# First four heads of a fused attention and MLP-Mixer kernel: loaded and scored in two pairs

## The chip, the cores and the metric

The kernel runs on one core of one Trainium2 chip. The metric is the device time in microseconds of one execution, the median of several runs; lower is better. The engines are TensorE (PE, with its weight loads as PEld), VectorE (DVE), ScalarE (ACT), GpSimd (POOL) and SyncE (SP), each with an instruction queue of its own.

## The reference

Eight batches of eight heads, 576 rows, 64 columns a head. Attention is causal by blocks of 64; its output, heads side by side (512 columns), goes through a token MLP with residual and then a channel MLP with residual. All inputs and the output are float32.

```python
scores = scale * np.matmul(q, k.transpose(0, 1, 3, 2))       # (8, 8, 576, 576)
scores = np.where(block_i >= block_j, scores, -1e9)          # blocks of 64
attn = np.exp(scores - scores.max(-1, keepdims=True))
attn = attn / (attn.sum(-1, keepdims=True) + 1e-09)
x = np.matmul(attn, v)            # then heads side by side: (8, 576, 512)
h = np.maximum(x.transpose(0, 2, 1) @ w_tok1, 0.0) @ w_tok2  # 576 -> 256 -> 576
u = x + h.transpose(0, 2, 1)
out = u + np.maximum(u @ w_ch1, 0.0) @ w_ch2                 # 512 -> 1536 -> 512
```

## The kernel before

The program is a list of steps, each made by `P.add` with an engine, a cost, the steps that it depends on and the PSUM banks that it takes and gives back. The order in which they stand on the engines was planned beforehand and is written out in a long string, `ORDER`: each word is a step's number, a letter for its engine (T for PE, A for ACT, D for DVE, P for POOL, S for SP) and letters for its banks. Nothing is reordered on the chip: each engine takes its steps in this order and waits for what a step needs.

For a batch and a group of four heads (`hg` 0 or 1), `load_qk` brings keys and queries into `qk_sb` as bfloat16, one head in 32 partitions (each partition holds 18 rows of the head). GpSimd's DMAs convert from float32 on the way. A transpose on DVE (32 by 32 blocks) then gives `kT` and `qT`. `score_set` forms one of three sets of score columns for several heads; each head works in its own 32 rows of TensorE. ACT takes the exponential of a set into `e_sb`. `tail` copies and clears the columns beyond the diagonal. `head_out` and `ends_out` multiply by the values, whose last column of ones gives the sums; DVE divides. Then come `token_up`, `first_uT` or `token_mix`, `channel_up` (or forms of it with seven products in place of eight) and the down projections, `first_down` for batch 0.

Batch 0 opens the program. Here is what stands at its start:

- `raise_clock` has PE multiply zeros, eleven times 512 columns (`WARM`), and then, where the plan has PE wait, 256 columns at a time (`KEEP`; 32 of them are in the order).
- The keys of the first four heads are loaded by SP as float32 in two pieces of nine blocks into a staging area in `gT` and cast by ACT (L395); their queries are loaded by GpSimd in three pieces (L431). Five transposes (L436) follow.
- `first_attention` scores the four heads of the first set at once; later sets are scored for two heads. The exponentials of two heads are one instruction on 1024 columns (L578), except two single ones (L728).
- GpSimd's queue issues, in order: the second group's queries and keys (L431), the next batch's (L413), values (L462), the token weights (L473), the identity matrix (`masks.py`), the channel weights `wc1_sb` (L496), and later `wc2_sb` (L505) among the loads of later batches. Memsets of the values' pad columns are on DVE.
- `channel_up` of batch 0 is one step of four matmuls for each of twelve tiles.

Of the kernel before, what the change touches and what calls it, by code (L numbers as in the profile page):

```python
# [27 lines left out]
class Plan:  # L28


    TURN = {
# [22 lines left out]
    def add(  # L54
# [4 lines left out]
        o = Op()  # L59
# [3 lines left out]
        o.mode, o.at, o.urgent, o.until, o.quick, o.stick = mode, at, urgent, until, quick, stick  # L63
        o.deps = list({id(d): d for d in deps if d is not None}.values())
# [33 lines left out]
    13S 9D 5D 16S 1D 43Ta 21P 2D 7D 11D 19P 10D 4D 3D 23P 31P 29P 14A 25P 15D 17A 33P 22D 18D 27P 20D 44Tb 249P 45Tb  # L98
    46Tb 47Td 24D 48Ta 49Ta 37P 50Ta 173Tsbc 36P 179Tt 174A 51Ta 52Ta 35P 53Ta 54Ta 55Ta 56Ta 57Ta 180A 34P 175D
    177Ts 26D 58Ta 59Ta 30D 176P 60Ta 178A 198Tt 252P 32D 61Ta 62Ta 40P 63Ta 199A 64Ta 28D 196Ts 42P 65Ta 66Ta 67Ta  # L100
    197A 230Tt 251D 258P 68Ta 69Ta 250D 70Ta 192A 39P 71Ta 211Ts 231A 189Td 38P 185Ta 186T 190D 181Tb 191D 182T 193A
    41P 232D 215Tt 212A 194D 154P 195D 72Tc 183D 73Tc 184D 200Td 74Tc 216A 75Tc 157P 213D 217Ts 8D 233D 254D 155P
    201T 218A 234Tt 187D 188D 12P 204Tb 214D 253D 205T 235A 255P 236Ts 206D 207D 156P 202D 227Ta 237A 203D 208Tb
    160P 223Tc 228D 224T 229D 219Td 159P 220T 225D 278Taefg 226D 161P 209D 210D 246Tc 221D 158P 222D 238Tb 281A 239T
    247D 162P 248D 242Td 279A 243T 240D 336Tc 163P 241D 282A 244D 334Ta 245D 280A 165P 260D 338Tb 335D 273Tdhfg 256D
    339A 342Ta 276A 340Tb 164P 277A 348Te 343T 341D 275A 337D 349T 399P 257D 351Tb 352T 350A 259D 263P 345Tc 344A
    346T 353D 274A 266Tfghe 262P 347D 267A 298Tabdc 261P 268A 356Tf 302A 265P 301A 360Tc 300A 357D 269A 358Td 361A
    354Tb 299A 270A 310Tcagf 355D 362Th 313A 271D 303D 272P 304D 312A 330D 264P 364Tb 363A 314A 396P 376Ta 311A 166P
    331D 370Te 359A 402P 365A 167P 305Tcdgh 371A 377D 366Tb 405P 309A 6D 168P 400D 308A 368Ta 401D 307A 306A 292Tf
    321Td 369A 293D 289Te 294D 286Tc 367A 322D 324Th 323D 374Tf 290D 291D 287D 288D 315Td 375A 325D 372Te 326D 398D  # L110
    283Tc 397D 373A 327Th 295Ta 316D 317D 570P 425Tbgfe 296D 328D 409P 329D 318Td 284D 427A 285D 387Th 319D 583P
    426A 320D 297D 428A 332D 420Tcdbg 410P 429A 388T 424A 412P 423A 479Ta 333D 408P 422A 421A 411P 477Tb 404D
    413Tdcfe 585P 478D 391Tg 414A 403D 415A 407D 573P 392T 417A 406D 480A 169D 586P 393T 416A 576P 485Tb 572D
    457Tdcae 486D 378Tf 458A 170D 461A 389T 459A 171D 460A 379T 172D 390A 445Tbdca 418D 394D 487Te 446A 419D 481Th
    448A 488D 380T 449A 482D 447A 430Tb 571D 452Tcage 431D 442Td 432D 734P 456A 450D 436Th 381D 579P 455A 433Tb
    495Te 454A 483Tf 434D 435D 491Tg 453A 443D 382Ta 444D 437D 492A 451D 575D 439Tb 484D 471Td 497Tg 496D 493Tc 440D
    468Tf 498A 441D 383T 472D 574D 494D 384T 438D 469D 470D 587Tbceg 577D 385A 489Th 501D 590A 578D 474Tf 589A 465Ta
    473D 591A 740P 462Te 475D 476D 505Tcd 588A 466D 737P 463D 467D 506Tf 490A 582P 592D 520Tbg 464D 508A 502D 521Ta
    584P 507A 511T 523A 522D 499Te 509Th 512A 500D 526T 580D 510A 599Teacf 503D 527A 513T 593D 504D 603A 515T 581D
    602A 524Tb 514D 601A 651Tf 516D 600A 525A 517D 594Tcahe 652D 528T 596A 739D 530T 595A 738D 518T 598A 653Ta 529D  # L120
    904P 597A 519D 535Tcb 531D 654A 619Tdfeh 735D 538A 533T 623A 736D 539Ta 622A 534D 536Th 901P 621A 541T 540D 743P
    620A 613Te 537D 659Tg 542A 624P 545T 614D 532A 615D 750P 626Tdcfh 660D 604Te 749P 546D 629A 661Tg 605D 628A 543T
    606D 630A 548T 662D 655Te 627A 544D 664S 631Tcfhg 549A 625D 547D 657Td 656D 632A 607Ta 633A 610Tb 658D 554Tce
    635A 608D 611D 663S 634A 612D 609D 616Tb 550D 555A 648Ta 763Tdfgh 551D 386S 556T 766A 395S 552D 765A 764A 560T
    553D 767A 557D 758Tdgfh 649D 650D 642Tc 759A 558Ta 643D 760A 741D 761A 644D 617D 645Td 762A 618D 669Tgc 665D
    646D 639Tb 647D 672A 684Tfh 640D 670Td 641D 559D 675T 671A 636Tb 745D 562T 676A 917P 744D 687A 666D 916P 561D
    690T 673Td 563D 747P 691A 564T 637D 674A 638D 568S 913P 667D 742D 751Tbagf 746P 565D 677T 914P 752A 679T 753A
    678D 566T 915P 754A 680D 755A 748P 795Tbadg 567D 756P 815Tf 907P 799A 668D 905D 798A 910P 688Te 902D 797A 685Td
    903D 796A 817Ta 689A 816D 686D 692T 818A 694T 693D 681A 783Tbdgf 695D 821Ta 785A 757D 819Te 822D 786A 682T 787A
    825Td 820D 699Tag 683A 826D 829S 823Tf 784A 777Tc 702A 824D 774Td 788P 697T 789P 778D 705T 779D 698A 775D 771Tb  # L130
# [1435 lines left out]
```

## Time and profile before

| | us |
|---|---|
| Median of three runs | 284.93 (284.62 to 286.27) |
| Profiled execution, its own time | 285.06 |
| Its span in the profile | 283.0 |
| PE busy | 275.3 |
| DVE busy | 245.1 |
| ACT busy | 172.3 |
| POOL busy | 69.3 |

The span is the time from the first to the last instruction; some 2 us lie around it. Times in the views are microseconds from the start of the span. In the chain of waits a row is start, length and what ran. In the timeline a row is start, length, engine, line, operation, output and input tile, shapes and count, and in brackets how long the engine was idle before it and what ended that. Rows of groups give, after the bar, the busy time and the mean of one in nanoseconds, then the idle time before them. Rows of DMA issues end with the us from issue to landing.

### The profile page before, as it was taken

How to read it: one execution, taken by the hardware profiler on the slowest of the kernel's cores; microseconds unless marked ns; L12 is line 12 of the kernel's file. 1: busy time of each engine (PE TensorE's matmuls, PEld its weight loads, DVE VectorE, ACT ScalarE, POOL GpSimd, SP SyncE). 2: the span in 40 equal slices, each digit the busy share in tenths (PEclk: the TensorE clock that was granted, in tenths of full speed). 3: DMA queues.
4: the chain of work that ended last, by engine and by line, in shares of the span. 5: the costliest groups of instructions: out<-in, count | busy, mean ns of one | idle time of the engine just before them, and what ended most of it. 6: DMA issues, size and time to landing. Idle time of an engine off the chain costs nothing.

```text
span 283.0 us, 9371 instructions
## 1 busy us (share of the span) xinstructions
PE 275.3 (97%) x4004; PEld 196.2 (69%) x4027; DVE 245.1 (87%) x533; ACT 172.3 (61%) x312; POOL 69.3 (24%) x115
## 2 busy tenths in 40 slices
PE   7899999999999999999999999999999999999995
PEld 3567565567776877887877767744488985468884
DVE  4678479799999988999999988899699898899975
ACT  3786887575998659787879687164514245734000
POOL 6895555511241090040535110000000000000000
PEclk9999999999999999999999999999999999999999
DMA  7999999994959599668599494030115603000436
GB/s 160 155 157 195 192 164 209 170 126 77 122 80 157 155 137 155 152 104 105 81 121 102 60 193 92 2 148 0 21 37 142 120 2 121 29 2 0 151 76 220
DMA packets 64776, 31.79 MB, mean 112 GB/s; under 512 B 53088, under 2 KB 55904, under 8 KB 64736
## 3 DMA queue, kind: packets, MB, share of 16 engines
q0 software_dynamic: 45040, 17.64, 54.0%
q1 hardware_dynamic: 19120, 12.78, 18.1%
q10 hardware_dynamic: 576, 0.79, 0.8%
q8 instruction: 31, 0.51, 0.7%
q14 instruction: 9, 0.07, 0.1%
HBM read 35.85 MB, written 9.44 MB: 160 GB/s over the span
## 4 chain that ended last, share of the span: by engine, by line
PE 85%; DMA 7%; POOL 3%; DVE 2%; issue 1%; ACT 0%; SPq 0%; DVEq 0%; POOLq 0%
PE late L1348 16%; PE mm L1348 10%; PE mm L1090 7%; PE late L1214 7%; PE late L1090 7%; PE mm L1214 6%; PE mm L560 6%; PE mm L608 4%; DMA wc_sb<-in_moe_w_ch_dram 4%; PE mm L802 3%; PE late L1443 2%; POOL vals L462 2%; PE mm L897 2%; PE late L608 2%; DMA vals<-in_v_dram 2%; PE mm L661 2%
## 5 line engine op out<-in xcount | busy, mean ns | idle before, releaser
L767 ACT ACTIVATE e_sb<-late 128x512 bf16<-128x512 f32 x85 | 48.4, 605 | 10.7 <-PE late L560 9.4
L767 ACT ACTIVATE e_sb<-mm 128x512 bf16<-128x512 f32 x83 | 47.1, 606 | 9.5 <-PE late L560 8.3
L436 DVE STREAM_TRANSPOSE qk_sb<-qk_sb 128x288 int32<-128x288 int32 (+1 forms) x65 | 41.3, 692 | 3.6 <-ACT qk_sb L395 1.9
L462 POOL DMA_DIRECT2D vals<-in_v_dram x45 | 36.8, 831 | 21.0 <-PE mm L661 8.8
L1348 PEld LDWEIGHTS <-gT 128*128 128x128 bf16 x288 | 27.7, 98 | 5.3 <-issue 0.9
L1348 PEld LDWEIGHTS <-sums 128*128 128x128 bf16 x288 | 27.7, 98 | 3.9 <-issue 0.7
L560 PEld LDWEIGHTS <-qk_sb 32*64 32x64 bf16 x1280 | 19.5, 104 | 13.7 <-issue 9.9
L560 PE MATMUL mm<-qk_sb 32*64 32x64 bf16 (+7 forms) x584 | 27.8, 287 | 0.3
L608 PEld LDWEIGHTS <-e_sb 128*128 128x128 bf16 x640 | 23.7, 97 | 5.1 <-issue 1.1
L560 PE MATMUL late<-qk_sb 32*64 32x512 bf16 (+7 forms) x556 | 26.4, 295 | 0.0
L1090 PEld LDWEIGHTS <-ws_sb 128*128 128x128 bf16 x192 | 18.2, 98 | 3.6 <-issue 0.9
L608 PE MATMUL mm<-vals,e_sb 128*128 128x65 bf16 x450 | 20.1, 193 | 0.1
L634 DVE TENSOR_TENSOR x_sb<-mm,rinv 128x256 bf16<-128x256 f32 x45 | 18.8, 422 | 1.3
L395 ACT COPY mm<-late 128x512 f32<-128x512 f32 (+1 forms) x15 | 8.7, 577 | 16.4 <-PE late L1348 8.0
L1348 PE MATMUL late<-wd_sb,gT 128*128 128x256 bf16 x144 | 17.7, 273 | 0.0
L1214 PEld LDWEIGHTS <-ws_sb 128*128 128x128 bf16 x96 | 9.3, 98 | 10.1 <-issue 0.2
L1090 PEld LDWEIGHTS <-wc_sb 128*128 128x128 bf16 x144 | 15.3, 114 | 1.2
L413 POOL DMA_DIRECT2D qk_sb<-in_k_dram x14 | 7.6, 543 | 33.3 <-DVE rinv L628 12.9
L788 ACT ACTIVATE gT<-mm 128x512 bf16<-128x512 f32 x19 | 11.3, 619 | 4.1 <-PE mm L1214 2.4
L788 ACT ACTIVATE gT<-late 128x512 bf16<-128x512 f32 x18 | 10.6, 601 | 4.4 <-PE late L1090 1.8
L1348 PE MATMUL late<-wd_sb,sums 128*128 128x256 bf16 x108 | 13.3, 273 | 0.0
L1214 PEld LDWEIGHTS <-wc_sb 128*128 128x128 bf16 x72 | 8.0, 113 | 7.0
(207 smaller groups left out, 644.0 us busy)
## 6 DMA issues: line engine op xcount, KB each, us to landing
out_dram<-o_sb SPq DMA_DIRECT2D x14, 512.0 KB, 3.6
qk_sb<-in_k_dram POOLq DMA_DIRECT2D x14, 288.0 KB, 4.4
qk_sb<-in_q_dram POOLq DMA_DIRECT2D x14, 288.0 KB, 5.3
vals<-in_v_dram POOLq DMA_DIRECT2D x28, 128.0 KB, 6.5
wc_sb<-in_moe_w_ch_dram POOLq DMA_DIRECT2D x8, 192.0 KB, 7.8
wc_sb<-in_moe_w_ch_dram POOLq DMA_DIRECT2D x3, 512.0 KB, 10.0
out_dram<-o_sb SPq DMA_DIRECT2D x5, 256.0 KB, 3.2
vals<-in_v_dram POOLq DMA_DIRECT2D x15, 64.0 KB, 5.0
```

Source lines behind the costliest of these rows:

```text
L395: nc.scalar.copy(dst, src)
L436: nc.vector.transpose(dst[:, 0:S, :] .rearrange("p s e -> p (s e)") .bitcast(I32) .rearrange("p (a k) -> p k a", k=NB)[:, k0:k1], raw2.bit ...
L462: nc.gpsimd.dma_start(out=t[128 - p : 128, J, hs, 0:64], in_=src)
L560: nc.tensor.matmul(out=home(n)[64 * half : 64 * half + 64, c : c + w], lhsT=bar[r, 0] if j is None else kT[i][r, 64 * j : 64 * j + 64, par ...
L608: nc.tensor.matmul(out=u[:, I, 0:65], lhsT=e[:, h, c : c + 128], rhs=vt[:, J, head, 0:65], start=(J == 0), stop=(J == I),)
L634: nc.vector.tensor_tensor(out=xt[:, 0:4, 64 * head : 64 * head + 64], in0=u[:, :, 0:64], in1=ri[:, 0:4].to_broadcast([128, 4, 64]), op=MULT,)
L767: nc.scalar.activation(dst, bank_of(x), EXP, scale=scale)
L788: nc.scalar.activation(dst, src, RELU)
L802: nc.tensor.matmul(out=ps, lhsT=w1_sb[:, c, tt : tt + 255 : 2], rhs=xt[:, c, cols], start=(c == 0), stop=False)
L1090: nc.tensor.matmul(out=bank_of(bank)[:, 256 * o_ : 256 * o_ + 256], lhsT=x(o_, m), rhs=y[:, :, m, :], start=opens, stop=m == 1, skip_group ...
L1214: nc.tensor.matmul(out=bank_of(bank), lhsT=x(m), rhs=y[:, :, m, :], start=first and m == 0, stop=m == 1, skip_group_check=not first,)
L1348: nc.tensor.matmul(out=bank_of(bank)[:, 256 * i : 256 * i + 256], lhsT=x[:, kk, 128 * i : 128 * i + 128], rhs=y[:, kk], start=first and i ...
```

## The change

The first group of batch 0 is brought in by a new function, `load_first`, as two pairs of heads. For heads 0 and 1, SP loads keys into partitions 0 to 63 and queries into partitions 64 to 127 of the staging area, in four pieces, the second half of the columns ahead of the first. One cast converts keys and queries together, in three pieces, on ACT or DVE as `ORDER` says. For heads 2 and 3, GpSimd loads keys and queries in the same layout with conversion, one DMA each. Transposes move 64 partitions each. A pair's scores depend on its own transposes alone, and every set of batch 0 is scored for two heads.

GpSimd's loads come behind the identity matrix and two memsets of the first value tiles, which were on DVE (`P.opening`). The filler matmuls are 512 wide (9 are in the order). `channel_up` is two steps of two matmuls each, each waiting for its own half of the weights and of `uT`. Every engine's order is written anew. The function `turn`, and the arguments `part` and `prev` of `score_set`, are added but not used in this program.

```diff
-    k_stage = gT[0].rearrange("p c s -> p (c s)").bitcast(FP32)
+    stage = gT[0].rearrange("p c s -> p (c s)").bitcast(FP32)[:, 0 : NB * D]
-    WARM, KEEP = 11, 110
+    WARM, KEEP = 11, 11
...
+        if o.engines == ("POOL",) and xfer is not None:
+            deps = [*deps, *self.opening]
...
-                "DVE", ("v", i), (-1e5 + 2, -40)[i],
+                ("POOL", "DVE")[i], ("v", i), (-1e6, -40)[i],
...
-        pads["ident"] = [P.add("POOL", 0.6, emit, (), -90)]
+        pads["ident"] = [P.add("POOL", 0.5, emit, (), -2e6)]
...
-                    out=bank_of(bank)[:, 0:256], lhsT=zeros[:, 0:128], rhs=zeros[:, 0:256],
+                    out=bank_of(bank), lhsT=zeros[:, 0:128], rhs=zeros,
...
+    def load_first():
+        hbm = [t[0, 0:4].rearrange("h (p k) d -> (h p) (k d)", p=32) for t in (k, q)]
+        raw = [t.rearrange("p k d -> p (k d)") for t in (kraw[0], qraw[0])]
+        halves = ((0, 9), (9, 18))
+        for k0, k1 in halves:
+            for n in range(2):
+                w = slice(D * k0, D * k1)
+                def emit(o, n=n, w=w):
+                    nc.sync.dma_start(out=stage[64 * n : 64 * n + 64, w], in_=hbm[n][0:64, w])
+                landed[k0, n] = P.add("SP", 0.44, emit, ...)
+        for n in range(2):
+            def emit(o, n=n):
+                nc.gpsimd.dma_start(out=raw[1][64 * n : 64 * n + 64, :], in_=hbm[n][64:128, :])
+            wide.append(P.add("POOL", 0.55 if n else 0.69, emit, ...))
+        def turn_pair(f, k0, k1, deps):
+            for n, t in enumerate((kT[0], qT[0])):
+                def emit(o, n=n, t=t):
+                    nc.vector.transpose(
+                        t[64 * f : 64 * f + 64, 0:S, :]
...
+                        raw[f][64 * n : 64 * n + 64].bitcast(I32).rearrange("p (k a) -> p k a", k=NB)[:, k0:k1],
+                    )
...
+        for k0, k1 in ((0, 9), (9, 14), (14, 18)):
+            def emit(o, w=slice(D * k0, D * k1)):
+                cast(o, raw[0][:, w], stage[:, w])
+            op = P.add(EVAC, ..., emit, [landed[9 * (k0 > 0), n] for n in range(2)], ...)
+            turn_pair(0, k0, k1, [[op], [op]])
+        for k0, k1 in halves:
+            turn_pair(1, k0, k1, [[ld] for ld in wide])
+        return pairs_ready[0] + pairs_ready[1]
...
-                if j == 0 and n == 0:
-                    note = {}
-                    early = [{"covers": True}, {"covers": True}]
-                    op = score_set(
-                        0, hg, n, range(4), ready[hg], prio - 0.05, [(SC, note)] + [(BANK, x) for x in early]
-                    )
...
+                op = score_set(0, hg, n, heads, ready[1] if hg else pairs_ready[f], prio + 0.1 * n, [(SC, note)])
...
+            for half in range(2):
+                ms = (2 * half, 2 * half + 1)
...
+                ready = [ld for n, ld in enumerate(wc1_ready[cc]) if n % NDM in ms]
+                op = P.add(
+                    "PE", mm_cost(512, 2), emit, [op] + uT_done[ms[0] : ms[1] + 1] + ready + g_war, ...
...
-    qk[0, 0] = load_qk(0, 0, pads["v", 0] + pads["w1"])
+    P.opening = pads["ident"] + pads["v", 0][:2]
+    qk[0, 0] = load_first()
```

Steps of the new order that the prediction speaks of: on SP the four loads; on POOL the identity, two memsets, pair 1's queries and keys, the second group's four loads with a memset among them, one value tile, then batch 1's first keys (which use the buffer of pair 0) and the value tiles; on PE, for batch 0, eight score sets, then the first value products, then the other four sets with value products between them, then batch 1's first scores.

More of the change, by code (lines that the diff above doesn't have):

```diff
@@ L175 @@
+    1458D 1463A 1482D 1485A
 """
@@ L553, in emit @@
         def emit(o):
-            opened = set()
-            for half, j, q, c, w, par in SETS[s]:
+            opened = {(half, n) for half in range(2) for n in range(len(heads))} if prev else set()
+            for half, j, q, c, w, par in SETS[s] if part is None else [x for x in SETS[s] if (x[3] < 320) == part]:
                 for n, h in enumerate(heads):
```

265 lines of the change are left out of this document (142 added, 123 removed).

## Prediction

> **What bounds the kernel now.** I read the page first, then busy time by stretches, the chain of waits of the first 21 us, the timeline there, the groups by form and the DMA issues. The page gives the bound:
>
> ```profile
> PE 275.3 (97%) x4004; PEld 196.2 (69%) x4027; DVE 245.1 (87%) x533; ACT 172.3 (61%) x312; POOL 69.3 (24%) x115
> ```
>
> The busy time by stretches (length, then busy us and instructions of PE, PEld, DVE, ACT, POOL) shows where TensorE is not bound by its own work:
>
> ```profile
> 0.00:8.00 8.00, 5.62 (x19) 2.31 (x20) 3.91 (x14) 2.63 (x3) 5.39 (x14) 1.00 0.84 163
> 8.00:21.20 13.20, 12.75 (x299) 8.35 (x298) 9.07 (x29) 11.56 (x13) 12.33 (x22) 1.00 1.47 154
> 21.20:279.30 258.10, 256.42 (x3688) 185.27 (x3708) 231.31 (x490) 158.10 (x296) 51.53 (x81) 1.00 0.70 108
> ```
>
> From 21.2 us to the end PE is covered, 256.42 of 258.10 us; only 1.7 us are open in all. Before 21.2 the picture deceives: until 8 us PE runs only warming matmuls, and after it part of its busy time is filler (L373). So the opening is where time can be had. Its chain of waits and its timeline:
>
> ```profile
> 1.22 4.51 DMA gT<-in_k_dram
> 5.74 0.68 ACT qk_sb L395
> 6.45 0.73 DVE qk_sb L436
> 7.46 0.53 POOL qk_sb L413
> 7.99 2.86 POOL vals L462 x4
> 14.75 5.14 DMA vals<-in_v_dram
> 19.93 0.65 PE mm L661 x20
> ```
>
> ```profile
> 0.75 0.88 SPq L420 DMA_DIRECT2D gT<-in_k_dram  x2
> 1.25 2.83 POOL L431 DMA_DIRECT2D qk_sb<-in_q_dram  x5 [0.79 <-POOLq L1550]
> 5.92 2.02 DVE L436 STREAM_TRANSPOSE qk_sb<-qk_sb 128x160 int32<-128x160 int32 x4 [0.79 <-DMA qk_sb<-in_q_dram]
> 8.00 0.33 PE L560 MATMUL sc<-qk_sb 32*64 32x320 bf16 x2 [1.18 <-DVE qk_sb L436]
> 8.76 5.03 ACT L578 ACTIVATE e_sb<-sc 128x1024 bf16<-128x1024 f32 x5 [2.35 <-PE sc L560]
> 15.54 5.01 ACT L578 ACTIVATE e_sb<-sc 128x1024 bf16<-128x1024 f32 x5
> 21.23 0.42 PE L560 MATMUL late<-qk_sb 32*64 32x512 bf16 x3
> ```
>
> Three limits follow each other. The first scores (8.00) wait for four transposes, which wait for queries that GpSimd loaded at 5.9, and for the second key load, at 5.7. Then ScalarE runs the exponentials of batch 0 without a pause from 8.76 to 20.55 (15.54 + 5.01). Beside it GpSimd issues the values; the last of them land at 19.89, and PE waits for them. At 21.23 batch 1's scores begin and PE is dense from there. **The time is, within small change, 258.7 us of dense PE plus the moment at which it starts plus the tail.** The totals of PE's matmuls, fillers aside, are the same in both programs, so only that moment and new gaps can change the time.
>
> **The change, part by part.**
>
> *First pair's loads.* Two SP loads of 288 KB become four of half the partitions, keys and queries of heads 0 and 1 (the same bytes on SP). The first half to be needed is columns 9 to 18 of both.
>
> ```profile
> gT<-in_k_dram SPq DMA_DIRECT2D x1, 288.0 KB, 2.9
> gT<-in_k_dram SPq DMA_DIRECT2D x1, 288.0 KB, 4.5
> L436 DVE STREAM_TRANSPOSE qk_sb<-qk_sb 128x288 int32<-128x288 int32 x11 | 7.0, 709 | 2.8 <-ACT qk_sb L395 1.9 <-DMA qk_sb<-in_k_dram 0.8
> L436 DVE STREAM_TRANSPOSE qk_sb<-qk_sb 128x160 int32<-128x160 int32 x1 | 0.5, 476 | 0.8 <-DMA qk_sb<-in_q_dram 0.8
> L436 DVE STREAM_TRANSPOSE qk_sb<-qk_sb 128x128 int32<-128x128 int32 x1 | 0.4, 397 | 0.0
> L395 ACT CAST qk_sb<-gT 128x576 bf16<-128x576 f32 x2 | 1.3, 672 | 3.0 <-DMA gT<-in_k_dram 3.0
> L634 DVE TENSOR_TENSOR x_sb<-mm,rinv 128x256 bf16<-128x256 f32 x4 | 1.7, 424 | 0.2
> L340 DVE MEMSET wd_sb<- 128x256 uint32 x1 | 0.3, 272 | 0.9 <-PEq L1550 0.9
> ```
>
> SP issues 0.47 us apart (0.75, 1.22), so the four go out at 0.75, 1.22, 1.69 and 2.16. With the first load's 2.9 us the second lands at 4.1; as its bytes are half, 3.65 is the other end, and I take 3.9. The fourth lands at 5.06 by 2.9 us; the worse end is 5.72, when the old second load of the same queue came in (1.22 + 4.5).
>
> [...]
>
> *Casts and transposes.* The first half's cast is shared: 320 columns on ACT (0.41, from 0.67 by columns; at most 0.67), 256 on DVE. A DVE cast of that shape isn't in the trace: between the memset's 0.27 and the 0.42 of a tensor_tensor; I take 0.3, as it reads one source. The transposes now move 64 partitions. Their cost lies between half and all of the full one; I take all, since in the three rows the time follows the columns (397, 476, 709). Four of them took 2.02 where the means add up to 2.29, so 0.07 each is overlap. DVE then runs: cast 3.9 to 4.2; four short ones 2 x (0.397 + 0.476) - 0.28 = 1.47, to 5.67; the two long ones need ACT's second cast, 5.06 + 0.67 = 5.73, and take 1.28: **7.0**. Ends: 6.7 (first landing at 3.65, DVE alone the limit) and 7.7 (last landing at 5.72). PE is ready earlier: the zeros' memset stands two small memsets later (0.28 us), so 11 warming matmuls and one filler end near 6.4. First scores at 7.05 against 8.00.
>
> *What this puts on DVE.* Ten transposes stand where five stood, about 3 us more. Pair 1's four come next, 7.0 to 9.6, with a small copy among them; its scores are wanted at about 10.0, after two exponentials. The second group's four then end near 12.3, wanted near 12.9. Both just hold; if not, ACT waits, up to 0.5 us.
>
> *ScalarE.* Twelve exponentials of a pair replace eleven and two single ones. Five take 5.01 to 5.03, 1.0 each. With 0.7 us for a first set of two heads (the set of four took 0.76) they run 7.75 to 19.75, against 20.55: **0.8 earlier**, if fed.
>
> *GpSimd.* The identity (before at 18.1) and three memsets of `vals` are put ahead of or among its loads:
>
> ```profile
> 18.11 0.20 POOL masks.py:197 MEMSET ident<- 128x128 bf16 x1
> 18.39 0.29 POOL masks.py:199 TENSOR_SCALAR_AFFINE_SELECT ident<-ident 128x128 bf16<-128x128 bf16 x1
> L591 POOL MEMSET e_sb<- 64x128 bf16 x1 | 0.2, 199 | 0.0
> L591 POOL MEMSET e_sb<- 64x256 bf16 x1 | 0.3, 306 | 3.0 <-DVE vals L586 3.0
> L462 POOL DMA_DIRECT2D vals<-in_v_dram x15 | 11.5, 782 | 0.6 <-issue 0.2
> vals<-in_v_dram POOLq DMA_DIRECT2D x1, 64.0 KB, 4.4
> vals<-in_v_dram POOLq DMA_DIRECT2D x1, 64.0 KB, 5.1
> ```
>
> Identity 0.57, the 64x528 memset 0.2 + 400 x 0.107/128 = 0.53, a small one 0.1: 1.2 us, part of it in the 0.79 us in which GpSimd waited anyway. Its first load goes out between 1.95 and 2.45 instead of 1.25; I take 2.2. But the old chain had GpSimd stand from 5.9 to 7.46 for the first transposes before batch 1's keys could go out, with all values behind it. In the new order eight issues precede that load, about 4.2 us (2.2 to 6.4, against transposes done at 7.0): it waits 0.6 instead of 1.6. The fifth value tile of the first group is then issued near 10.2 and lands 4.4 later at 14.6 (14.2 without that wait). PE asks for it behind its eighth score set, at 7.75 + 6.0 + 0.6 = 14.35: a wait of 0 to 0.3. The last tile of the second group stands at 14.0 to 14.3 and lands 5.1 later, **19.1 to 19.4 against 19.89**. PE waits there for a short stretch, with only head outputs behind it.
>
> *Filler and order.* Twenty-five fillers after 8.00 become eight of twice the width.
>
> ```profile
> 9.08 0.94 PE L373 MATMUL mm<-wd_sb 128*128 128x256 bf16 x7
> 8.00:21.20 13.20, 3.86 (x25) 1.88 (x25) 1.00 1.47 154
> ```
>
> Seven take 0.94 with an end of 0.27, 0.11 each, so the twenty-five are 2.7 us. They fill waits, so nothing is won by dropping them; their cover is that PE must stay at the clock 1.00 that the stretches show, and no gap of the sum is above 1 us.
>
> *Sum.* The last exponential ends at 19.75, one end-of-row product follows, batch 1's scores start at 20.1 instead of 21.23: 1.1 us. About as much of batch 0's value products is left then as before (three heads against two and an end row). I take 0.1 back for the waits named: 1.0 us. The channel weights' first use is split into halves; the same matmuls, so nothing there by itself, and if a weight is late it only shortens a wait. The profiled execution took 285.06 with span 283.0; 285.06 - 1.0 = 284.06, and as it lies 0.13 over the median of the runs, 284.93, **283.9**. Its own range, from the ends 6.7 and 7.7 and the values, is 283.3 to 284.7.
>
> **The rivals.**
>
> *Nothing arrives earlier (0.25): 284.9.* The halves queue on the same engines, the fourth lands at 5.72, first scores at 7.7; GpSimd's delayed start gives values at 19.9. For it: the 4.5 us row; against: GpSimd's loads, which ran beside that one, now start about a microsecond later.
>
> *Slower: second-layer weights come behind PE (0.22): 286.4.* In the new order two key/query loads instead of one stand between the first and second load of `w_ch2`, all behind a tail step of GpSimd that waits for exponentials:
>
> ```profile
> 34.80 0.31 POOL L591 MEMSET e_sb<- 64x256 bf16 x1 [2.99 <-DVE vals L586]
> 37.71 9.98 DMA wc_sb<-in_moe_w_ch_dram
> 47.74 1.02 PE late L1443 x4
> 21.20:60.00 38.80, 38.21 (x669) 22.80 (x670) 29.74 (x71) 28.67 (x56) 19.58 (x30) 1.00 1.42 186
> ```
>
> PE began its product at 47.74, 0.05 after the landing. One load of 288 KB more ahead is 295 KB / 186 GB/s = 1.6 us later, and PE comes 1.0 earlier: up to 2.6 us, so 284.06 + 2.6 - 0.13 = 286.5, at the median about 286.4. It decides if PE has less than that of other work; counted over PE's instructions, the order puts that product some 2.5 us later behind batch 1's first scores, which is why I give it less than the main case. Should value loads behind these be late too, it passes 288; that holds half of this case.
>
> *More than said (0.1): 282.2.* The new order also closes the 1.7 us open in the dense stretch: 283.9 - 1.7. Nothing in the trace says it would.
>
> **How the numbers follow.** Main case 0.43. A difference of 1% (2.8 us) is what a measurement of this kernel can tell from none. Faster by that needs 282.1: most of the last rival, 0.07. Slower by it is the upper half of the weights case, 0.11; the rest, 0.82, is within. The range goes from 282.3 to 286.6, leaving out the far halves of both outer rivals.
>
> **What would show it.** Right: first scores near 7.05; first exponential near 7.75 and last end near 19.75; batch 1's scores near 20.1; GpSimd's wait before batch 1's keys below 1 us; last values before 19.5. Wrong: first scores after 7.7, ACT gaps over 0.3 us among the twelve, a PE gap over 0.5 us after 21 us, or a product with `w_ch2` that starts on a landing.

## The result, and the profile after

The changed kernel takes 295.59 us (median of six runs, 294.48 to 296.21) against 285.60 of the kernel before on the same chip: **3.4% slower**, ratio 1.0338 (95% interval 1.0288 to 1.0388). The forecast was 283.9 us, within 282.3 to 286.6. Ratios, here and below, leave out runs more than 1.5% above the fastest of their kernel, so that of a kernel whose clock falls in some runs only they mostly describe the others. The profiled execution took 296.21 us with a span of 294.4. The page of after, engine totals and granted clock by fortieths of the span, then the clock row of before:

```profile
PE 281.8 (96%) x3979; PEld 198.6 (67%) x4004; DVE 242.5 (82%) x519; ACT 176.4 (60%) x319; POOL 73.6 (25%) x126
PEclk9655799999999999999999999999999999999998
```

```profile
PEclk9999999999999999999999999999999999999999
```

TensorE's totals say nothing: 96% busy, against 97% before. The clock row says all: from the second to the fifth slice it is 5 to 7 where before it was full. By the stretches that the forecast used (us, busy us and instructions of PE, PEld, DVE, ACT, POOL, then clock, DMA share, GB/s):

```profile
0.00:8.00 8.00, 4.87 (x12) 1.58 (x12) 2.47 (x9) 2.02 (x3) 5.36 (x16) 1.00 0.75 153
8.00:21.20 13.20, 10.35 (x150) 5.42 (x154) 8.74 (x18) 7.57 (x9) 10.46 (x16) 0.54 1.17 125
21.20:60.00 38.80, 37.70 (x658) 23.89 (x656) 25.83 (x75) 25.28 (x46) 18.11 (x29) 0.85 1.03 151
```

At 0.54 a score set that takes 0.64 us at full clock (9.12 to 9.76 in the run with two memsets, section 5) took 1.05 (9.92 to 10.97), and ScalarE waits for it: 9 instructions of it stand in the stretch that held 13 before. Stretches of 0.1 us find the edges (busy us and instructions of PE alone, then clock, DMA share, GB/s; so in all stretches below):

```profile
9.02:9.12 0.10, 0.00 (x0) 1.00 1.39 189
9.12:9.22 0.10, 0.00 (x0) 0.50 1.36 173
32.91:33.01 0.10, 0.10 (x7) 0.50 0.89 154
33.01:33.11 0.10, 0.10 (x8) 0.98 0.85 154
```

**TensorE ran at half clock from 9.12 to 33.01 us.** The timeline shows what came ahead of it (start, us, engine, line, operation, tiles, count, idle time before and what ended it):

```profile
5.90 0.38 PE L374 MATMUL mm<-wd_sb 128*128 128x512 bf16 x1
9.92 0.47 PE L604 MATMUL sc<-qk_sb 32*64 32x320 bf16 x2 [3.64 <-DVE qk_sb L426]
4.46 1.28 ACT L396 ACT_TABLE_LOAD   x1 [4.46 <-DMA gT<-in_k_dram]
11.05 1.94 ACT L623 ACTIVATE e_sb<-sc 128x1024 bf16<-128x1024 f32 x2 [2.65 <-PE sc L604]
10.41 0.53 POOL L467 DMA_DIRECT2D qk_sb<-in_k_dram  x1 [4.40 <-DVE qk_sb L426]
```

TensorE stood idle 3.64 us between the one filler left there and the first scores at 9.92 (before: 1.18 us, first scores at 8.00). The chain of waits says why they were late (start, us, what):

```profile
2.01 0.60 SPq L413
...
2.65 5.00 DMA gT<-in_k_dram
...
7.72 0.68 ACT qk_sb L396
...
8.43 0.71 DVE qk_sb L426
...
9.15 0.72 DVE qk_sb L426
...
9.92 1.11 PE sc L604 x14
```

The fourth of SP's loads was 5.00 us in flight and landed at 7.64. The span grew by 11.4 us, in three places: batch 1's first scores at 30.47 instead of 21.23 (9.2); from there to TensorE's last product 259.8 us instead of 258.6, with the half clock lasting 2.5 us into it (1.2); and from that product to the end 4.15 us instead of 3.17 (1.0).

### The profile page after: what moved, and what is told of

The parts are those of the page before. It is cut to its first block, busy times and chain, and to the rows that moved or that the text cites. A ratio compares the mean times of both kernels' runs of the same rounds, so it can differ in the third digit from the quotient of the medians.

```text
span 294.4 us, 9340 instructions
## 1 busy us (share of the span) xinstructions
PE 281.8 (96%) x3979; PEld 198.6 (67%) x4004; DVE 242.5 (82%) x519; ACT 176.4 (60%) x319; POOL 73.6 (25%) x126
## 4 chain that ended last, share of the span: by engine, by line
PE 93%; DVE 2%; DMA 2%; issue 1%; SPq 1%; ACT 1%; ACTq 0%
PE mm L1384 14%; PE late L1384 12%; PE late L1126 7%; PE mm L604 7%; PE late L1250 6%; PE mm L1250 6%; PE mm L1126 5%; PE mm L654 5%; PE sc L604 4%; PE mm L830 3%; PE late L1504 3%; PE mm L925 3%; PE late L654 3%; PE late L604 2%; PE late L830 2%; PE late L1053 2%
## 5 line engine op out<-in xcount | busy, mean ns | idle before, releaser
L480 DVE STREAM_TRANSPOSE qk_sb<-qk_sb 128x288 int32<-128x288 int32 x60 | 38.8, 700 | 3.3 <-PE sc L604 1.7
L604 PEld LDWEIGHTS <-qk_sb 32*64 32x64 bf16 x1280 | 21.9, 110 | 20.4 <-issue 12.1
L396 ACT COPY mm<-late 128x512 f32<-128x512 f32 (+1 forms) x22 | 12.4, 566 | 22.8 <-PE late L1384 9.6
L623 ACT ACTIVATE e_sb<-sc 128x1024 bf16<-128x1024 f32 x12 | 12.2, 1023 | 8.7 <-PE sc L604 8.7
L604 PE MATMUL sc<-qk_sb 32*64 32x512 bf16 (+7 forms) x160 | 12.5, 435 | 5.0 <-DVE qk_sb L426 3.6
L632 POOL COPY vals<-e_sb 128x256 bf16<-128x256 bf16 x11 | 5.4, 498 | 47.1 <-ACT e_sb L795 34.1
L1126 PEld LDWEIGHTS <-wc_sb 128*128 128x128 bf16 x144 | 15.2, 113 | 1.1
L674 DVE RECIPROCAL rinv<-mm 128x4 f32<-128x4 f32 x42 | 7.1, 173 | 9.1 <-PE mm L654 8.9
L467 POOL DMA_DIRECT2D qk_sb<-in_q_dram x14 | 7.9, 565 | 25.2 <-DVE rinv L674 15.7
L940 DVE TENSOR_TENSOR u_sb<-mm,x_sb 128x512 bf16<-128x512 f32 x18 | 11.8, 680 | 2.7 <-PE mm L925 2.3
```

What stands on the lines that cost most here:

```text
L396: nc.scalar.copy(dst, src)
L480: nc.vector.transpose(dst[:, 0:S, :] .rearrange("p s e -> p (s e)") .bitcast(I32) .rearrange("p (a k) -> p k a", k=NB)[:, k0:k1], raw2.bit ...
L604: nc.tensor.matmul(out=home(n)[64 * half : 64 * half + 64, c : c + w], lhsT=bar[r, 0] if j is None else kT[i][r, 64 * j : 64 * j + 64, par ...
L623: nc.scalar.activation(dst, sc[SC.index(note["pool"])][:, :, cols], EXP, scale=scale)
L1126: nc.tensor.matmul(out=bank_of(bank)[:, 256 * o_ : 256 * o_ + 256], lhsT=x(o_, m), rhs=y[:, :, m, :], start=opens, stop=m == 1, skip_group ...
```

## The experiments

Each ran beside the kernel before on the same chip. "Weighted share", first used in the run with thin matmuls, is a sum over a window: each matmul's 512 columns count 0.215 us at full clock (16 warming matmuls took 3.62 us, the last being 0.39 long) and twice that at half clock (the score matmuls of 512 columns of after at 30.47 and 30.90 stand 0.43 apart); this is multiplied by the matmul's tile as a share of 128*128, the largest tile in the views (a score matmul is 32*64, an eighth), and divided by the window. The page of after has 3979 matmuls to 4004 weight loads, so some matmul records seem to be missing, and the share is good to a few hundredths.

### 1. Fill the idle time: 18 warming matmuls instead of one (e1_fill18)

```diff
-            def emit(o, bank=bank):
+            def emit(o, bank=bank, reps=18 if n == 0 else 1):
+                for _ in range(reps):
...
```

> One edit: the single warming matmul that stands between the first eleven and the first scores is issued 18 times instead of once (18 x 512 columns, about 0.2 us each at full clock), so that TensorE has work over the 3.64 us in which it stood idle from 6.28 to 9.92. Loads, casts and transposes are untouched. Theory A (the idle gap takes TensorE to half clock, and that is the loss): the granted clock stays at 1.00 from 8 to 33 us, the first scores stay late, at about 9.9, but the score sets run at 0.6 instead of 1.06 us, the exponentials at 1.0 instead of 1.5 us each, batch 1's scores begin at 22.5 to 23 instead of 30.47, and the time is 286 to 288. Theory B (the late first scores and the new order cost the time themselves, and the half clock only goes with the idle time behind them): batch 1's scores still come after 28 and the time stays above 293.

Six runs from 288.25 to 296.57 us, median 291.48, against 284.53: neither theory's range. The three with a mean clock of 0.998 to 1.000 took 288.25 to 289.17 us (ratio of these 1.014, 1.0069 to 1.021), the three with 0.963 to 0.969 took 293.79 to 296.57. The first scores came at 11.38 in the profiled run, as the fourth load landed at 9.11. That run (296.57) lost its clock too, later and without a long gap. Stretches of 3.41 us (PE busy, clock):

```profile
6.81:10.23 3.42, 3.42 (x17) 1.00 1.17 161
10.23:13.64 3.41, 1.83 (x48) 1.00 0.25 21
13.64:17.05 3.41, 3.21 (x44) 0.50 1.47 144
```

It follows that a gap of 3.64 us is not needed; here gaps of 0.89 and 0.69 us went with the fall. The time from fall to rise is a multiple of 3.413 us in the profiles of after (9.12 to 33.01, 23.89, seven), of this run (13.64 to 34.12, 20.48, six) and of section 2, where stretches of 2 us give it to a few hundredths (8.88 to 32.76, 10.63 to 31.12, 8.32 to 32.20). The windows below are therefore of that length and laid by each profile's own clock records, whose edges lie differently in each. In the one ahead of this fall PE was not idle but busy 1.83 of 3.41 us.

### 2. What made the first scores late: table load, GpSimd's loads, SP's issues

Table load first in the order (e2_table): `0A`, a one-column exponential near the end of ScalarE's order, moved to the front; the load of ScalarE's function table (ACT_TABLE_LOAD) then comes ahead of the first landing instead of behind it.

> One edit: ScalarE's table load (1.28 us) is placed first in the order, ahead of all else, instead of behind the first landing, where it stood at 4.46. Theory A (the first scores are set by the fourth load's landing at 7.64, through the second cast of ScalarE and the two long transposes): the first cast moves from 5.76 to about 4.5, the short transposes with it, but the second cast stays at 7.7, the first scores at 9.9, the idle gap at 3.6, the clock at 0.50 from 10 us, and the time at 295 to 296. Rival (the table load is what made the first scores late): the first scores come at about 8.6, the gap is 2.4, and if that is short enough for the clock the time is about 286.

296.62 us in one run. The table load ran at 0.75, and the first scores came at 9.75 behind a gap of 3.59: theory A, with the time a little over its range. The table load's place in the change is harmless, since the fourth load is later.

GpSimd's loads 2.2 us later (e3_poollate):

```diff
             make_identity(nc, ident)
+            for _ in range(4):
+                nc.gpsimd.memset(o_sb[2][:, 0, :], 0.0)
```

> One edit: four more memsets of a buffer that is not in use yet, about 1.5 to 2.5 us of work, stand on GpSimd behind the identity, so that its own loads go out at about 3.5 to 4 instead of 1.81. Theory A (SP's four half-width loads land late, 6.1 and 7.6, because GpSimd's loads of pair 1 share the DMA engines from 3.3 us on): third and fourth landing at 5.0 to 5.7, first scores at 7.5 to 8.2, idle gap under 2 us, clock at 1.00, and the time near 285 to 287. Rival (half-width loads are slow by themselves, in issue and in the queue): third and fourth landing stay at 6.1 and 7.6 within 0.4, first scores at 9.6 to 9.9, clock at half, time 295 to 298.

294.40 us in one run. The loads of SP in the view by tile, first of after and then of this run (issue to landing):

```profile
DMA to landing us min/median/max: 2.8/3.6/5.0
```

```profile
L415 SPq DMA_DIRECT2D gT<-in_k_dram x2: 585/591/597, 1.4 to 2.7; - x2
DMA to landing us min/median/max: 2.9/2.9/2.9
```

All four took 2.9 us once GpSimd's loads went out from 4.02 instead of 1.81, the third and fourth landing at 4.95 and 5.60: shown, GpSimd's earlier loads made the fourth late here (7.64 in after). What the loads share, no run tells apart. The issue itself stayed at 0.59 us. First scores at 8.68, later than theory A had them, because now the table load (4.38) was the last to end ahead of the first cast. The clock still fell, at 10.63, although the idle time was only 1.98 and 0.70 us, so this one run lies just below the 294.48 to 296.21 of the changed kernel.

Half of SP's loads issued by ScalarE (e4_actq): `(nc.scalar if w.start == 0 else nc.sync).dma_start(...)`.

> One edit: the two loads of the second half (columns 0 to 9 of keys and of queries) are issued by ScalarE's queue instead of SP's, so that SP issues two loads and ScalarE two, side by side. Theory A (SP's issue of 0.64 us per load makes the last ones late): third and fourth load go out about 1.3 us earlier, the fourth lands at 6.0 to 6.5, first scores at 8.3 to 8.8, gap about 2.3. Rival (the engines' sharing sets the landing): the fourth lands after 7.0 whoever issues it, and the first pair lands later too, first scores after 9.3, gap over 3, clock at half, time 294 to 297.

294.75 us in one run. The fourth landed at 6.48, but the first half's second load only at 4.97, and behind it the table load: first scores 9.33, clock 0.50 from 8.32. The fourth load is as theory A has it; the first scores, the gap (3.45) and the time are as the rival has them.

### 3. Hold the clock, and take it from the kernel before

16 warming matmuls ahead of the first scores, three behind the first set (e6_held; loads and casts as in the change):

```diff
+            def emit(o, bank=bank, reps={0: 16, 1: 3}.get(n, 1)):
+                for _ in range(reps):
...
-    51Tb 31D 81Ts 157P 30D 44P 85Tt 82A 28D 52Ta 41P
+    51Tb 31D 81Ts 52Ta 157P 30D 44P 85Tt 82A 28D 41P
```

> Two edits, both of warming matmuls alone: 16 of 512 columns instead of one ahead of the first scores (until about 10.0), and three instead of one directly behind the first score set, where the run with 18 ahead of the scores still stood idle for 0.69 us. Loads, casts, transposes and the rest of the order are as in the changed kernel. Theory A (TensorE's clock is halved when a window of 3.4 us has too much idle time, somewhere between the 35% of before and the 46% of the run with 18): with every window above that, the clock stays at 1.00 in all runs; first scores at about 10 to 10.5, exponentials 1.0 us apart, batch 1's scores at 22.5 to 23.5, time 286 to 288 with little spread between runs, against 288 to 297 with 18 matmuls. Theory B (half clock comes from the late scores in another way, the load on the array or the new order): the clock still falls between 9 and 14 us and the time stays above 291 in most runs.

Ratio 1.0167 (1.0114 to 1.0221); the four runs took 288.58, 288.87, 290.51 and 297.05 us, so the small spread was missed: in the last the mean clock was 0.958, against 0.994 to 0.998 in the others. In the profiled run (288.87) the clock held:

```profile
8.00:21.20 13.20, 12.50 (x247) 1.00 1.22 129
21.20:60.00 38.80, 37.77 (x664) 1.00 1.35 184
```

First scores at 9.89, as late as in after, but batch 1's at 24.02 instead of 30.47. **With loads and their landings as in the change, the clock is 6.4 of the 9.2 us by which batch 1 starts late.**

The kernel before with its warming matmuls cut to 8 columns (b1_nofill):

```diff
-                    out=bank_of(bank)[:, 0:256], lhsT=zeros[:, 0:128], rhs=zeros[:, 0:256],
+                    out=bank_of(bank)[:, 0:8], lhsT=zeros[:, 0:128], rhs=zeros[:, 0:8],
```

> The kernel before, with one edit: each of its warming matmuls behind the first eleven is cut from 256 to 8 columns, so that they hardly occupy TensorE. Nothing depends on their result. Theory A (idle time alone halves the clock): the idle time ahead of the first scores grows from 1.18 to about 1.8 us and the waits between the score sets open by 0.1 to 0.9 us each, the clock falls to 0.50 between 9 and 14 us although first scores still come at 8.0, batch 1's scores begin at 26 to 29 instead of 21.23, and the time is 290 to 294. Theory B (the loss belongs to the new loads and order): the time stays within 1 us of 284.9.

287.02 us in one run against 284.28. The clock fell as theory A has it, and the scores-to-batch-1 time grew from 13.23 to 15.96 us; the total is lower than expected, because the first scores happened to come at 6.99 and the half clock ended at 24.48 (mean clock 0.974). But its windows don't fit idle time:

```profile
4.00:7.41 3.41, 1.69 (x52) 1.00 1.15 164
7.41:10.83 3.42, 2.80 (x84) 1.00 1.30 179
10.83:14.24 3.41, 3.41 (x77) 0.50 1.74 171
```

Half idle, and the clock stayed; 82% busy, and it fell. The second window holds score matmuls, 32*64 or an eighth of the largest tile each, and the fillers of 8 columns. That gave the theory of the weighted share: 0.36 in the first, 0.23 in the second.

### 4. Busy, but thin (e9_thin)

The held kernel, its warming matmuls on 32 rows and 64 columns:

```diff
-                        out=bank_of(bank), lhsT=zeros[:, 0:128], rhs=zeros,
+                        out=bank_of(bank)[0:64, :], lhsT=zeros[0:32, 0:64], rhs=zeros[0:32, :],
```

> The kernel with 16 and three warming matmuls, which held the clock, with one edit: all its warming matmuls behind the first eleven use 32 rows and 64 columns of the array instead of 128 and 128. They have the same 512 streamed columns each, so TensorE is occupied for the same time. Their result is used nowhere. Theory A1 (the gate counts how much of the array works: over the windows of 3.4 us of ten profiles, streamed columns weighted with rows and columns in use were 0.32 of full or less in each window after which the clock fell, 0.36 or more in each after which it stayed): the weighted share of the window behind the first eleven is 0.1 to 0.3, and the clock falls to 0.50 at about 9 to 10 us, before the first scores, though TensorE has hardly a gap; time 291 to 297. Theory A2 (the gate counts idle time): the clock stays at 1.00 and the time is 288 to 290.

292.93 us in one run, as A1 has it. Stretches, then the timeline:

```profile
2.85:6.26 3.41, 3.41 (x10) 1.00 1.01 226
6.26:9.67 3.41, 3.41 (x17) 1.00 1.27 179
9.67:13.09 3.42, 3.42 (x49) 0.50 0.49 76
```

```profile
6.21 3.70 PE L375 MATMUL mm<-wd_sb 32*64 32x512 bf16 x16
9.77 0.47 PE L605 MATMUL sc<-qk_sb 32*64 32x320 bf16 x2
```

(The first row's 1.00 stands ahead of the first clock record: its matmuls began 0.43 us apart, twice the 0.215 of full clock.) TensorE was busy through the whole window from 6.26, 3.41 of 3.41 us, and the clock was 0.50 behind it: shown, a fall without idle time. The weighted share of that window is 0.12. The windows at full clock during batch 0, all behind which the clock fell (two alike left out, 0.13 and 0.22) and the three lowest behind which it stayed:

| kernel, window (us) | PE busy of 3.41 | weighted share | clock behind it |
|---|---|---|---|
| after, 5.71 | 0.57 | 0.11 | half |
| thin, 6.26 | 3.41 | 0.12 | half |
| GpSimd late, 7.22 | 1.25 | 0.14 | half |
| 18 matmuls, 10.23 | 1.83 | 0.21 | half |
| before without fillers, 7.41 | 2.80 | 0.23 | half |
| four memsets, 14.92 | 2.29 | 0.32 | half |
| six edits, 14.61 | 2.54 | 0.35 | half |
| before without fillers, 4.00 | 1.69 | 0.36 | full |
| three memsets, 13.54 | 2.74 | 0.36 | full |
| two memsets, 6.27 | 1.93 | 0.38 | full |

Sorted by busy time the outcomes are mixed; by the weighted share these windows part between 0.35 and 0.36. The theory was formed on ten profiles (before, after, sections 1 to 3 and the first two runs of section 5); the seven taken later, the thin run's first, all fit. What the chip itself goes by, and whether it has such a bound, no run shows. In after the clock stayed at half behind six windows of 0.27 to 0.64 and was back at full behind the seventh, at 0.88 (29.60 to 33.01), with batch 1's denser start.

### 5. With the clock held, what is left

Four edits (e7_best4): GpSimd's four memsets, table load first, `reps={0: 5, 1: 3}`, `52Ta` moved as above. Then the same with two memsets and six matmuls (e8_best2).

> Four edits together: the four memsets that hold GpSimd's loads back to about 4.0, the table load placed first, five warming matmuls ahead of the first scores and three behind the first set. Theory A (with the landings at 4.3 and 5.6 and the first cast no longer behind the table load, the first half of the forecast comes true, and the clock is held): first scores at 7.5 to 8.0, first exponential at 8.3 to 8.7, clock 1.00 throughout, time 283.5 to 286. Rival (GpSimd's start, 2.2 us later, hits the values): the last values land after 21, TensorE waits for them before batch 1, whose scores begin at 21.5 to 23 although the exponentials end at about 20.5, and the time is 285.5 to 287.5.

> As the kernel with four memsets, but with two (GpSimd's loads from about 2.9) and six warming matmuls ahead of the first scores. Theory A (the order of the loads decides): SP's fourth load lands between 5.6 and 6.5, first scores at 7.8 to 8.8, values about 1 us earlier than with four memsets, batch 1's scores at 21 to 21.8, clock 1.00, time 284 to 286. Rival (any overlap with GpSimd's loads costs the whole 2 us): fourth landing after 7, first scores after 9.2, time 286 to 288 or, where the clock falls, 291 to 297.

Four memsets: 290.75 us, ratio 1.0201 (1.0152 to 1.0251), over both ranges. First scores 7.83, first exponential 8.55, as theory A has them (the prediction had 7.05 and 7.75); but GpSimd's late start left TensorE waiting 1.01 us for values at 15.32, and the clock fell at 18.34. Two memsets: 287.97 us, ratio 1.0125 (1.0086 to 1.0164), clock 1.00 throughout, fourth load at 6.85, first scores 9.12, batch 1 at 23.75: close to the rival. The last values had landed only at 23.15: they queue on GpSimd behind batch 1's key load, which waits for the first transposes (9.61). So that load was moved (e10_vals: `157P` behind `43P`), and then with three memsets (e11_best3: behind `40P`).

> The kernel with two memsets ahead of GpSimd's loads (first scores 9.12, batch 1's 23.75, 287.97 us), with one edit: the load of batch 1's keys, which GpSimd can't issue before the first transposes are done (9.61 there), is moved behind the four value loads that stood behind it. Theory A (with the clock held, the values that queue behind this load are what puts batch 1's start 2.5 us later than before): values issued from 7.05 on, the last one landing at about 20.3 instead of 23.15, the gap of 0.69 at 22.5 and that of 0.67 among the exponentials gone, batch 1's scores at 22.0 to 22.7, time 286 to 287.2. Rival (the later first exponential, 9.84 against 8.76, sets all that follows): batch 1's scores stay at 23.3 to 23.8, time 287.5 to 288.5.

> Both remedies: three memsets hold GpSimd's loads to about 3.4, the table load is first, the clock is held by six and three warming matmuls, and batch 1's key load is moved behind three value loads. Theory A (three causes, clock, landing and values, make up the loss): SP's fourth load lands at 5.6 to 6.3, first scores at 7.8 to 8.5, exponentials from 8.6 to 20.8, last value at 20 to 21, batch 1's scores at 21.2 to 21.8, time 284.3 to 286, level with before. Rival (something else in the new order costs as well): batch 1's scores come when forecast and the time is still over 286.5, or the exponentials have further gaps and batch 1 comes after 22.5.

Key load moved: 286.32 us, ratio 1.0051 (1.0035 to 1.0066), last value 21.42, batch 1 at 22.25: time and batch 1 are as theory A has them, although the exponentials kept a gap of 1.10. But half of the 1.5 us by which batch 1 came earlier is the fourth load, which happened to land at 6.11 instead of 6.85: first scores at 8.38 instead of 9.12. From there to batch 1 the edit saved 0.8 us (13.88 instead of 14.64). Three memsets: fourth load 5.49, batch 1 at 21.75 as forecast, yet 286.61 in the profiled run, so by its mark of 286.5 the rival holds: something else costs as well. Median 288.76 (286.61 to 291.12), ratio 1.0114 (1.0024 to 1.0204): two of the four runs lost part of the clock (mean 0.979 and 0.982, 290.86 and 291.12 us); the profiled run's lowest window, 0.36 above, stands next to a fall at 0.35. TensorE's waits, of the run with two memsets and of that with three:

```profile
PE mm L657 <- DMA vals<-in_v_dram: 0.7, 1, 0.7
PE mm L710 <- DMA vals<-in_v_dram: 0.2, 1, 0.2
```

```profile
PE mm L710 <- DMA vals<-in_v_dram: 0.7, 1, 0.7
PE sc L607 <- DVE w_sb L341: 0.3, 1, 0.3
```

Six edits (e12_fix): besides, one more warming matmul behind the second score set, `42P` and `45P` change places, `157P` behind `43P`, `1464A` and `1463A` become `1464S` and `1463S` (output writes by SP).

> The kernel with three memsets, early table load and held clock, with three edits more: on GpSimd the fifth value tile of the first group changes places with the first of the second group and batch 1's key load stands behind all five of the first group; one warming matmul more behind the second score set; and two of the last five output writes are issued by SP instead of all five by ScalarE. Theory A (values and closing writes are what is left of the loss): no wait for values among the score sets (0.67 us at 15.37 there), exponentials from 8.5 to 20.4, batch 1's scores at 20.8 to 21.4, the end 3.1 to 3.6 us behind TensorE's last product, time 284.2 to 285.4. Rival (the wait only moves to DVE, where batch 1's key transposes stand ahead of the copies and reciprocals, and the end stays as it is because the last write is slow whoever issues it): batch 1 after 21.5, end 4.0 behind the last product, time over 286.

289.65 us, ratio 1.0172 (1.0127 to 1.0218). The rival: the wait moved to DVE, whose transposes of batch 1's keys now waited 1.94 us for their load with batch 0's memsets behind them, and the clock fell at 18.02.

```profile
PE mm L657 <- DVE e_sb L640: 0.9, 1, 0.9
```

Those transposes moved behind the end-row divisions (e13_dve: `159D 158D` behind `99D`):

> The kernel with six edits, with one more: DVE's two transposes of batch 1's keys stand behind the copies, memsets and end-row divisions of batch 0 that they held up (a key of batch 1 isn't needed before its scores). Theory A (that wait, and the clock that it cost, are what is left): no idle time of TensorE over 0.4 us behind the first scores, clock 1.00, exponentials from 8.6 to 20.4, batch 1's scores at 20.7 to 21.4, time 284 to 285.5, level with before. Rival (the new order has more such waits): the clock falls again or batch 1 comes after 21.8, time over 286.

286.46 us, ratio 1.0052 (1.0026 to 1.0078), 12 runs. Clock 1.00, exponentials from 8.75 to 20.80, batch 1 at 21.89: by the marks (batch 1 after 21.8, time over 286) the rival, without a fall of the clock. TensorE waited 0.73 us ahead of a value product:

```profile
PE mm L657 <- DMA w_sb<-in_moe_w_tok_dram: 0.7, 1, 0.7
```

```profile
18.29 0.72 DVE L483 STREAM_TRANSPOSE qk_sb<-qk_sb 128x288 int32<-128x288 int32 x1 [0.45 <-DMA qk_sb<-in_q_dram]
20.59 0.42 DVE L683 TENSOR_TENSOR x_sb<-mm,rinv 128x256 bf16<-128x256 f32 x1
21.06 0.46 PE L657 MATMUL mm<-vals,e_sb 128*128 128x65 bf16 x10 [0.73 <-DMA w_sb<-in_moe_w_tok_dram]
```

The view names the load of a token weight, but this product reads values and exponentials, and that load went out at 16.66 with 6.7 us to landing, so it came down after the wait had ended. What ended 0.05 us ahead of the product is DVE's division (L683, to 21.01), and ahead of that stood DVE's transposes of batch 1's queries, which had waited 0.45 us for their load. So most likely the wait is on DVE again, as the rival has it; no run moved those transposes.

So the new order, with every remedy found, comes within about 0.5% of before and not below it.

The closing writes. In after all of the last five go through ScalarE's queue, in before one of them through SP's. The DMA views of the ends, before, after, and with two on SP again (KB, us to landing):

```profile
out_dram<-o_sb ACTq DMA_DIRECT2D x2, 128.0 KB, 1.8
```

```profile
out_dram<-o_sb ACTq DMA_DIRECT2D x1, 128.0 KB, 2.3
```

```profile
out_dram<-o_sb ACTq DMA_DIRECT2D x1, 128.0 KB, 1.7
```

The end came 3.17, 4.15 and 3.66 us behind TensorE's last product: half of the microsecond between before and after is the last write's 2.3 instead of 1.8. Why it takes longer behind four others of the same queue, and where the other half goes, stays open.

The same two edits on the kernel before: key load behind two values (b2_keys), then behind four and the transposes later (b3_keys).

> The kernel before, with one edit: on GpSimd the load of batch 1's keys, at 7.46, where it stood idle for 1.58 us until the first transposes were done, changes places with the two value loads behind it. Theory A (values queue behind that load, there too): value loads from 5.9 on, last landing at 18.4 to 18.9 instead of 19.89, the wait of 0.45 us for them at 19.48 gone, batch 1's scores at 20.8 to 21.1 instead of 21.23, time 0.2 to 0.45 us less (ratio 0.9985 to 0.9993). Rival (the last exponential, which ends at 20.55, sets batch 1's start): values earlier, batch 1's scores within 0.1 of 21.23, time the same within 0.15 us.

> The kernel before, with two edits: on GpSimd batch 1's key load stands behind all four value loads that stood behind it, and DVE's two transposes of these keys stand behind the end-row and copy steps of batch 0. Theory A (the values of batch 0 and the DVE steps behind the keys are what TensorE waits for in the opening of before): no wait for values at 14 us, the one at 19.48 (0.45) gone or under 0.2, batch 1's scores 0.4 to 0.8 us earlier relative to the first scores than the 13.23 of before (8.00 to 21.23), time 0.4 to 0.9 us less, ratio 0.997 to 0.9985. Rival (the last exponential or the queries' loads, which the edit pushes back, set batch 1's start): ratio within 0.001 of 1.

Ratios 0.9973 (0.9946 to 1.0001) and 1.0038 (1.0014 to 1.0062). The first may be a gain, which its interval doesn't settle, and two of its twelve runs lost part of the clock (mean 0.982, 289.15 and 289.64 us). Its profile doesn't show the gain either: batch 1 came at 20.81, but the first scores at 7.04, so that the way from one to the other was 13.77 us, longer than the 13.23 of before. The second is slower by about 0.4%. Its profile has a wait of 1.80 us at 47.76 for `w_ch2`, the place that the forecast's rival with late weights named:

```profile
37.83 11.69 DMA wc_sb<-in_moe_w_ch_dram
```

The load went out 0.12 us later than before (37.71) and was 1.7 us longer in flight (9.98 before). So it wasn't pushed back in GpSimd's queue; why it took longer stays open.

## Why the prediction was wrong

**Filler and order: the step that failed.** "No gap of the sum is above 1 us" was the condition, and the cover of every other term. The text itself had all that was needed: PE ready near 6.4, a first-score end of 7.7, only one filler left ahead of it. That is a gap of 1.3 us in its own worst case, and 3.64 in fact. The condition was also the wrong one: gaps of 0.89 and 0.69 us went with a fall in the run with 18 matmuls, and the thin run lost its clock without a gap. What the fillers had held up was the weighted share: 0.46 or more in every window of before from 5.88 until batch 1, 0.11 in the window of after behind which the clock fell. The price of a lost clock, 6.4 us by the held kernel, was not in the sum, in no rival and not in the range. The forecast weighed no wait as long as the 3.64 us of after.

**First pair's loads: mis-sized.** SP's issues took 0.59 us and stood 0.64 apart, not 0.47; the fourth load landed at 7.64, not 5.06, and beyond the worse end of 5.72. The rival with late halves had the late landing, but its argument against, that GpSimd's loads start later, was wrong twice: they started at 1.81, ahead of SP's third and fourth, and the forecast's own 2.2 would not have helped: from 2.86, in the runs with two memsets, the fourth still landed at 6.1 and about 6.9. The bound was taken from one load's 4.5 us, with one load of SP beside GpSimd's instead of three. With GpSimd's loads out from 4.02 only, the four loads to the two partition halves each landed 2.9 us after their own issue, 0.64 us apart: that the halves queue on the same engines, as that rival has it, does not show at this spacing. And the 8.00 to be beaten was the latest of the four profiles of before and its variants: in the other three both loads took 2.8 to 3.1 us, where the second had taken 4.5, and the first scores came at 6.99 to 7.37 without any change to the loads in front of them.

**Casts and transposes: the costs were right.** Casts 0.46 and 0.29 us (0.41 and 0.3 forecast), and a transpose of 64 partitions cost what one of 128 did (0.41 for 128 columns, 0.71 for 288). The table load between landing and first cast was overlooked and cost nothing here, though 1.3 us once the loads were early (4.38 to 5.64 in the run with GpSimd's loads late).

**ScalarE.** With the clock held, twelve exponentials took 12.05 us (8.75 to 20.80; 12.0 forecast), but the eleven and two of before had taken 11.79: pairing saves nothing there. All of the gain had to come from the earlier landing, and in no run of the new order were the first scores ahead of 7.79, against 7.05 forecast. From there to batch 1 the sum had 13.05 us; in the three runs that came closest it took 13.87 to 13.97. So the order would not have gained its microsecond with the clock at full speed either.

**GpSimd: the wait went the other way**, 4.40 us instead of 0.6, because it hangs on the same transposes. (The 19.89 of before isn't its last value's landing, as the prediction has it, but that of the last but one, for which TensorE waited; the last came at 20.13.) That the values stand behind it was said; that a late first transpose therefore counts twice, in the scores and in the values, was not.

**The tail** was taken as unchanged and was 1.0 us longer. **Late weights** did not come in this kernel, where everything was later, but did in the last run on the kernel before. **The range:** the lower end of its own range, 283.3, doesn't follow from the ends that it names; 6.7 instead of 7.0 and no wait give 283.5.

## What to carry to other kernels

Matmuls that seem to do nothing may be holding the clock: in the kernel before, with the fillers cut to 8 columns, it went to 0.50 at 10.83 us and the time from 284.28 to 287.02. Before they are removed or shortened, add up, for windows as long as the profiles show (3.41 us here), what share of the largest tile is at work, and ask what happens if one load is 2 us late. Here the clock stayed at full behind every window of batch 0 with a share of 0.36 or more and fell behind every one with 0.35 or less; in after it came back behind one of 0.88, while the stage of score matmuls ahead of it had 0.64 at most, so one bad window cost over 6 us. The load that was split in four on a queue of its own landed at 7.64 with GpSimd's loads out from 1.81 and at 5.60 with them out from 4.02: bound such a landing by all loads issued up to then.

## What the runs showed of the hardware that was not expected

- The clock fell behind a window with 3.41 of 3.41 us busy (thin, weighted share 0.12), and stayed at full behind one with 1.69 busy (before without fillers, share 0.36): in these windows the outcome went with the weighted share, not with TensorE's idle time. That holds for the windows of this case alone.
- 144 KB loads took 2.9 us to land with GpSimd's loads out from 4.02, and up to 5.0 (6.5 in the run with 18 matmuls) with them out from 1.81, at the same issue time of 0.59 us; one 288 KB load of before took 0.41 us to issue.
- First scores of the kernel before came at 8.00, 6.99, 7.04 and 7.37 us in four profiles with the same loads in front (before, without fillers, and the two with the key load moved), so a single profile's landing is uncertain by about a microsecond.
